# Eight columns of g times w_out's scale: from the end of a VectorE chain to ScalarE

## The chip, the cores and the metric

The kernel runs on one core of a Trainium2 chip. The metric is the device time of one execution in microseconds, as the median of several runs; the kernel before has three. The profile is one more execution of the same program, taken by the hardware profiler. The engines are named as the profile names them: PE is TensorE (PEld its weight loads), DVE is VectorE, ACT is ScalarE, POOL is GpSimd, and SP is SyncE, which issues the transfers here. Every engine takes its own instructions strictly in the order in which the program lists them.

## What is computed

An attention whose keys and values are averaged over blocks of eight rows feeds one dense block with a SoLU and a layer norm in its middle:

```python
k_p = k.reshape(B, H, Sp, 8, D).mean(axis=3)          # B, H, S, D = 8, 8, 576, 64
v_p = v.reshape(B, H, Sp, 8, D).mean(axis=3)
attn = softmax(q @ k_p.T / sqrt(D))
x = (attn @ v_p).transpose(0, 2, 1, 3).reshape(4608, 512)
h = x @ w_in                                          # 512 x 1024
solu = h * softmax(h)
ln = (solu - mean(solu)) / sqrt(var(solu) + 1e-6) * g_ln
out = ln @ w_out                                      # 1024 x 512
```

All inputs and the output are float32. `g_ln` has 1024 values, one for each row of `w_out`, and the kernel multiplies it into `w_out` while that is prepared.

## The kernel before

The 4608 rows are worked in 36 tiles of 128 rows. Products on PE are done in float16, with each operand split into a high and a low float16 part, so that three products (high by high, low by high, high by low) stand for one in float32. A tile passes these stages: the transposed q (`qT`) times the transposed keys (`scores`, PSUM tile `sc`), the softmax, the transposed weights (`eT`) times the values (`av`, PSUM tile `xp`), the split of x (`x_hi` on ACT, `x_lo` on DVE, tile `xT`), the first dense product (`mm1`, L892, PSUM tile `hp`), the SoLU (`h_max` and `h_nb` on DVE, `h_exp` on ACT, `z_mul` on DVE), centring and splitting (`z_hi`, `z_cen` on ACT, `z_lo` on POOL), the transposes by DMA (`zT`), the second dense product (`mm2`, L1024, PSUM tile `op`) and the eviction (`o_evac`, L1032, tile `osb`). The raw keys and values are halved three times on POOL (`pool_kv`, L348, tiles `kr`, `vr`, `kp`, `vp`).

Before the tiles can use `w_out`, it is scaled. `weight("wo", ...)` lists the steps. `w_exp`, `w_shift`, `w_abs` and `w_tail` decode and bound the raw weights. `wo_scale` (from L632) is a chain of small DVE instructions on columns of 128 x 1: it rounds the bounds of w_out and g to powers of two, multiplies them into `pwo` (L637), takes the reciprocal `sw_wo` (L642), changes `pwo` for the use in the evictions (L643), and ends with `sg_wo` (L647). `sg_wo` is g's 1024 values, laid out as 128 partitions by 8 columns (`g_sb`), times the one scale `sw_wo`: column d scales the d-th eighth of `w_out`'s rows. The readers of `sg_wo` are `w_hi` (L667, eight ACT instructions that write the high part of `wo`) and `w_lo` (L696, eight DVE instructions that write the low part from two SBUF tiles, the raw weights and the high part). The first tile's `mm2` needs the high parts first and the low parts in its last third.

The instructions are not placed by a scheduler at build time. `op` numbers every step in the order in which the code lists them, and the table `ORDER` at the head of the file says in which order these numbers are emitted; each engine gets its steps in that order. The numbers do not change with the data.

Three more names come up in what follows. `a_max` (L367, tile `amx_q`) takes the largest magnitude of a batch's q on DVE, and `spread` (L376, PSUM tile `gq`) copies it to all partitions on PE, in the same PSUM buffer that `xp` uses. `hp` has two PSUM buffers, `op` has one.

Of the kernel before, what the change touches and what calls it, by code (L numbers as in the profile page):

```python
# [12 lines left out]
AF = mybir.ActivationFunctionType  # L13
ALU = mybir.AluOpType
# [166 lines left out]
def kernel(  # L181
# [10 lines left out]
    nc = tc.nc  # L192
# [49 lines left out]
    g_sb = const.tile([P, CO], F32, name="g_sb")  # L242
# [1207 lines left out]
```

## Time and profile before

| | us |
|---|---|
| median of 3 runs (lowest, highest) | 484.06 (483.23, 486.1) |
| the profiled execution, whole | 485.99 |
| its span, first to last instruction | 484.3 |
| PE busy in the span | 445.5 (92%) |
| ACT, DVE, POOL busy | 353.9, 346.4, 346.5 |

The span is what the trace covers; 1.69 us of the profiled execution lie outside it. The profiled execution took 1.93 us more than the median of the three runs. PE is the busiest engine by far, so the first question to any other engine's time is whether PE waited for it. The trace tells for each instruction when it began and how long it took, for idle time what ended it, and for each stretch the clock that was granted to PE, as a share of full speed.

### The profile page before, as it was taken

The page shows a single profiled execution, that of the slowest core. Times are in us where ns is not written, and L with a number is a line of the kernel's source. Part 1 is how long each engine was busy: PE and PEld are TensorE (multiplying, and loading weights), DVE is VectorE, ACT ScalarE, POOL GpSimd, SP SyncE. Part 2 cuts the span into 40 slices and gives each one's busy share as a digit, 9 for nine tenths or more (in the row PEclk, how much of TensorE's full clock was granted, in tenths as well). Part 3 has the DMA queues.
Part 4 walks back from the last instruction along what each step waited for, and adds up shares of the span by engine and source line. Part 5 has one row for each costly group of instructions (what it writes and reads, how often), then busy time and mean ns, then how long its engine had stood idle before and what let it go on. Part 6 is the DMA issues. An engine that isn't in the chain of part 4 may idle for free.

```text
span 484.3 us, 9040 instructions
## 1 busy us (share of the span) xinstructions
PE 445.5 (92%) x3100; PEld 231.6 (48%) x3100; DVE 346.4 (72%) x835; ACT 353.9 (73%) x593; POOL 346.5 (72%) x489
## 2 busy tenths in 40 slices
PE   0269869999999999999999999999999999999996
PEld 0124424455455545555555555555545555545462
DVE  3999997679768867777567886688557787782620
ACT  1899769758976597776896689667876679667741
POOL 7254926877999988998889568986999547535340
PEclk9999979999999999999999999999999999999999
DMA  8999934799889989798977988789997656635351
GB/s 277 376 342 222 255 70 103 132 233 231 186 202 233 198 177 223 180 201 223 193 164 182 199 182 199 196 180 211 206 199 154 162 121 120 132 77 137 87 137 59
DMA packets 201390, 89.14 MB, mean 184 GB/s; under 512 B 177664, under 2 KB 186112, under 8 KB 200832
## 3 DMA queue, kind: packets, MB, share of 16 engines
q1 hardware_dynamic: 201344, 88.57, 78.5%
q8 instruction: 24, 0.39, 0.4%
q14 instruction: 22, 0.18, 0.1%
HBM read 36.70 MB, written 9.44 MB: 95 GB/s over the span
## 4 chain that ended last, share of the span: by engine, by line
PE 83%; DVE 6%; ACT 4%; DMA 3%; POOL 2%; issue 1%; SPq 0%; ACTq 0%; DVEq 0%
PE op L1024 36%; PE hp L892 36%; PE xp L860 6%; PE sc L770 3%; DMA qr<-in_q_dram 2%; DVE sg_wo L647 1%; DMA eT<-e 1%; DVE amx_q L367 1%; ACT ab_wi L554 1%; POOL e L839 0%; DVE e L810 0%; ACT u_wi L531 0%; DVE sc L795 0%; ACT sc L791 0%; DVE xT L872 0%
## 5 line engine op out<-in xcount | busy, mean ns | idle before, releaser
L892 PE MATMUL hp<-wi,xT 128*128 128x512 f16 x864 | 198.3, 382 | 2.0 <-ACT xT L868 1.9
L1024 PE MATMUL op<-wo,zT 128*128 128x512 f16 (+1 forms) x888 | 197.0, 373 | 0.8 <-ACT osb L1032 0.6
L892 PEld LDWEIGHTS <-xT 128*128 128x128 f16 x864 | 83.2, 99 | 99.0 <-issue 3.7
L1024 PEld LDWEIGHTS <-zT 128*128 128x128 f16 x888 | 84.7, 98 | 90.7 <-issue 1.0
L959 POOL TENSOR_TENSOR z<-z,z 128x512 f16<-128x512 f32 x71 | 81.9, 1165 | 52.2 <-ACT z L946 51.9
L902 DVE TENSOR_REDUCE m<-hp 128x1 f32<-128x1024 f32 x36 | 44.0, 1222 | 29.6 <-PE hp L892 29.5
L839 POOL TENSOR_TENSOR e<-e,e 128x512 f16<-128x512 f32 x36 | 42.2, 1172 | 23.1 <-ACT e L832 22.9
L348 POOL TENSOR_TENSOR vr<-vr 128x512 f32<-128x512 f32 (+3 forms) x48 | 47.4, 994 | 10.4 <-DMA vr<-in_v_dram 9.7
L951 ACT ACTIVATE z<-z,sz 128x1024 f16<-128x1024 f32 x36 | 41.2, 1145 | 17.7 <-DVE z L937 17.5
L913 ACT ACTIVATE z<-hp,nb,Hb 128x1024 f32<-128x1024 f32 x32 | 38.4, 1198 | 15.5 <-DVE nb L905 14.7
L937 DVE SCALAR_TENSOR_TENSOR z<-hp,rs,z 128x1024 f32<-128x1024 f32 x36 | 46.1, 1280 | 3.7 <-ACT z L913 2.3
L348 POOL TENSOR_TENSOR kr<-kr 128x512 f32<-128x512 f32 (+3 forms) x48 | 40.8, 860 | 3.5 <-DMA kr<-in_k_dram 3.0
L781 DVE TENSOR_REDUCE mx<-sc 128x8 f32<-128x576 f32 x36 | 27.1, 754 | 22.2 <-PE sc L770 21.9
L946 ACT ACTIVATE z<-z,sz 128x1024 f32<-128x1024 f32 x36 | 41.1, 1144 | 0.7
L1032 ACT ACTIVATE osb<-op,f 128x512 f32<-128x512 f32 (+1 forms) x37 | 24.7, 668 | 20.0 <-PE op L1024 12.4
L860 PEld LDWEIGHTS <-vb 128*128 128x128 f16 x640 | 35.3, 98 | 8.5 <-DMA eT<-e 0.7
L860 PE MATMUL xp<-eT,vb 128*128 128x128 f16 (+1 forms) x640 | 38.2, 214 | 0.2 <-DMA eT<-e 0.2
L972 ACT ACTIVATE junk<-z 128x1024 f16<-128x1024 f32 x36 | 37.7, 1047 | 0.2
L751 POOL TENSOR_TENSOR q<-qr,q 128x512 f16<-128x512 f32 x28 | 32.3, 1156 | 7.2 <-ACT q L741 7.2
L795 DVE TENSOR_REDUCE sc<-sc 128x8 f32<-128x576 f32 x36 | 27.4, 762 | 13.5 <-ACT sc L791 13.3
L770 PE MATMUL sc<-kT,qT 128*128 128x72 f16 (+1 forms) x640 | 25.6, 201 | 11.9 <-DMA qT<-q 7.9
L868 ACT ACTIVATE xT<-xp 128x512 f16<-128x512 f32 x36 | 21.3, 592 | 16.5 <-PE xp L860 16.2
(232 smaller groups left out, 588.8 us busy)
## 6 DMA issues: line engine op xcount, KB each, us to landing
kr<-in_k_dram SPq DMA_DIRECT2D x16, 512.0 KB, 4.5
qr<-in_q_dram SPq DMA_DIRECT2D x16, 512.0 KB, 4.8
vr<-in_v_dram SPq DMA_DIRECT2D x16, 512.0 KB, 4.9
out_dram<-osb SPq DMA_DIRECT2D x31, 256.0 KB, 3.3
wor<-in_moe_w_out_dram SPq DMA_DIRECT2D x4, 1024.0 KB, 7.5
wo<-in_moe_w_in_dram SPq DMA_DIRECT2D x2, 1024.0 KB, 9.6
wir<-in_moe_w_in_dram SPq DMA_DIRECT2D x2, 1024.0 KB, 13.2
out_dram<-osb SPq DMA_DIRECT2D x10, 128.0 KB, 2.3
```

The costliest lines, as they stand in the source:

```text
L348: nc.gpsimd.tensor_tensor(out=dst, in0=src[:, :, :n], in1=src[:, :, n : 2 * n], op=ALU.add)
L770: nc.tensor.matmul(sc[lo:hi, h // HB, (h % HB) * SP : (h % HB + 1) * SP], lhsT=t["qT"][:, h, lo:hi], rhs=bat[b]["kT"][:, x, hc], start=(x ...
L839: nc.gpsimd.tensor_tensor(out=m[:, 1], in0=e_pair(i)[:, :, :P], in1=m[:, 0], op=ALU.subtract)
L860: nc.tensor.matmul(xp[:, c, lo:hi], lhsT=vb[b % 2][:, x, c].rearrange("p j d -> p (j d)"), rhs=eT[:, e, lo:hi], start=(n == 0), stop=(n == 3),
L892: nc.tensor.matmul(hp[:, f], lhsT=xT[:, xt, c], rhs=wi[:, wt, c, f * 512 : (f + 1) * 512], start=(part == 0 and n == 0), stop=(part == 2 a ...
L902: nc.vector.tensor_reduce(out=small(i, "m"), in_=tl[i]["hp"], axis=AX.XY, op=ALU.max)
L913: nc.scalar.activation(z, t["hp"], AF.Exp, bias=t["nb"], scale=hsc(i, 0), accum_out=small(i, "se"))
L937: nc.vector.scalar_tensor_tensor(out=t["z"], in0=t["hp"], scalar=t["rs"], in1=t["z"], op0=ALU.mult, op1=ALU.mult, accum_out=small(i, "sz"),)
L946: nc.scalar.activation(t["zf"], t["zf"], AF.Identity, bias=t["sz"], scale=-float(DFF))
L951: nc.scalar.activation(t["z16"][:, 0], t["zf"], AF.Identity, bias=t["sz"], scale=-float(DFF))
L959: eng.tensor_tensor(out=t["z16"][:, 1, fs], in0=t["zf"][:, fs], in1=t["z16"][:, 0, fs], op=ALU.subtract)
L1024: nc.tensor.matmul(op_, lhsT=zT[:, zt, c], rhs=wo[:, wt, c, cols(hf)], start=(part == 0 and n == 0), stop=(part == 2 and n == len(todo) - 1),)
```

## The change

`sg_wo` leaves `wo_scale` and becomes a step of its own, `wo_cols`, on ACT. It reads `g_sb` and the scale `sw_wo`, which `wo_scale` now keeps. All other steps stay as they were. Because there is one step more, every step behind it has a number higher by one in `ORDER`; apart from that and the new step's place the table is the same. The line of the table with the new step (117) and the edits of the code:

```diff
-    299, 300, 302, 225, 301, 259, 483, 484, 345, 344, 260, 123, 347, 303, 227, 485, 486, 146,
+    300, 301, 303, 226, 302, 260, 484, 485, 346, 345, 117, 261, 124, 348, 304, 228, 486, 487,
...
         nc.vector.tensor_scalar(
             out=pwo, in0=pwo, scalar1=-(2.0**-8), scalar2=None, op0=ALU.mult
         )
+        wst["wo"]["sw"] = sw
+
+    def wo_cols():
         sg = const.tile([P, CO], F32, name="sg_wo")
-        nc.vector.tensor_scalar(out=sg, in0=g_sb, scalar1=sw, scalar2=None, op0=ALU.mult)
+        nc.scalar.activation(sg, g_sb, AF.Copy, scale=wst["wo"]["sw"])
         wst["wo"]["s"] = sg
...
-            op("dve", 1.2, t_sum + 0.8, wo_scale, r=[("g2", nm), ("gg2",)], w=[("ws", nm)])
+            n = op("dve", 1.2, t_sum + 0.8, wo_scale, r=[("g2", nm), ("gg2",)], w=[("ws", nm)])
+            op("act", 0.2, t_sum + 2.0, wo_cols, r=[("g",)], w=[("ws", nm)], after=[n])
```

On DVE, at the end of w_out's scale, before (`amx_q` is the magnitude of q, `xT` the split of x, `m` the maximum of a row of `hp`; a number behind a name is its buffer):

```order
L642 RECIPROCAL sw_wo<-pwo 128x1
L643 TENSOR_SCALAR pwo<-pwo 128x1
L647 TENSOR_SCALAR sg_wo<-g_sb,sw_wo 128x8
L367 TENSOR_REDUCE amx_q<-qr_480 128x1
L872 SCALAR_TENSOR_TENSOR xT_670<-xp_653,xT_670 128x512
L902 TENSOR_REDUCE m_684<-hp_556 128x1
```

The same place after:

```order
L642 RECIPROCAL sw_wo<-pwo 128x1
L643 TENSOR_SCALAR pwo<-pwo 128x1
L367 TENSOR_REDUCE amx_q<-qr_480 128x1
L875 SCALAR_TENSOR_TENSOR xT_668<-xp_651,xT_668 128x512
L905 TENSOR_REDUCE m_682<-hp_556 128x1
```

The instruction between `pwo` and `amx_q` is gone, and nothing else moved.

On ACT, at the high parts of w_out, before (`e_1_97` is the split of the softmax, `z_758` the exponentials of the next tile):

```order
L868 ACTIVATE xT_670<-xp_653 128x512
L834 ACTIVATE e_1_97<-e_608 128x2x32
L667 ACTIVATE wo<-wor_370,sg_wo 128x512 x2
L667 ACTIVATE wo<-wor_314,sg_wo 128x512 x2
L667 ACTIVATE wo<-wor_322,sg_wo 128x512 x2
L667 ACTIVATE wo<-wor_282,sg_wo 128x512 x2
L913 ACTIVATE z_758,se_759<-hp_556,nb_694,Hb_362 128x1024
```

The same place after:

```order
L871 ACTIVATE xT_668<-xp_651 128x512
L837 ACTIVATE e_1_97<-e_608 128x2x32
L650 ACTIVATE sg_wo<-g_sb,sw_wo 128x8
L670 ACTIVATE wo<-wor_370,sg_wo 128x512 x2
L670 ACTIVATE wo<-wor_314,sg_wo 128x512 x2
L670 ACTIVATE wo<-wor_322,sg_wo 128x512 x2
L670 ACTIVATE wo<-wor_282,sg_wo 128x512 x2
L916 ACTIVATE z_758,se_759<-hp_556,nb_694,Hb_362 128x1024
```

`sg_wo` stands directly ahead of the first of its readers; PE, POOL and SP have the rows that they had.

## Rows read from the trace of the kernel before

**Rows 1.** Windows: stretch, its length, busy us by engine, PE's clock, DMA share, GB/s

```profile
71.00:110.00 39.00, 38.02 (x296) 19.70 (x295) 27.90 (x68) 29.31 (x52) 27.72 (x40) 1.00 0.73 154
110.00:450.00 340.00, 339.69 (x2422) 177.14 (x2421) 249.43 (x621) 257.44 (x440) 269.73 (x370) 1.00 0.82 180
```

**Rows 2.** Waits of PE: who waited for whom, us in total, times, longest

```profile
PE gq('b', 1)_686 L376 <- DVE xT L872: 5.5, 1, 5.5
```

**Rows 3.** Chain that ended last, 57 to 66 us: start, us, what

```profile
57.35 6.05 DVE sg_wo L647
...
64.52 0.61 DVE xT L872
...
65.17 0.37 PE gq('b', 1)_686 L376 x2
```

**Rows 4.** Timeline of PE, 57 to 83: start, us, instruction, count [idle before, releaser]

```profile
57.80 1.90 PE L892 MATMUL hp<-wi,xT 128*128 128x512 f16 x8 [0.85 <-ACT xT L868]
...
65.34 5.84 PE L892 MATMUL hp<-wi,xT 128*128 128x512 f16 x16
...
75.42 3.62 PE L892 MATMUL hp<-wi,xT 128*128 128x512 f16 x16
...
82.32 1.03 PE L1024 MATMUL op<-wo,zT 128*128 128x512 f16 x4
```

**Rows 5.** Windows around PE's stand, columns as in rows 1

```profile
59.70:63.00 3.30, 0.00 (x0) 0.00 (x0) 3.30 (x1) 0.00 (x0) 3.30 (x6) 1.00 0.98 172
...
65.20:69.80 4.60, 4.60 (x13) 1.76 (x13) 4.57 (x15) 4.60 (x9) 0.00 (x0) 0.50 0.01 4
```

**Rows 6.** Timeline of DVE at the same place, columns as in rows 4

```profile
57.27 6.13 DVE L647 TENSOR_SCALAR sg_wo<-g_sb,sw_wo 128x8 f32<-128x8 f32 x1
```

**Rows 7.** Line L801, an instruction of the same size: ns shortest/median/longest

```profile
L801 DVE TENSOR_SCALAR sc<-sc x36: 154/174/175, 27.5 to 430.4; 128x8 f32<-128x8 f32 x36
```

**Rows 8.** Timeline of POOL, 56 to 66, first and last ones, columns as in rows 4

```profile
56.59 1.14 POOL L839 TENSOR_TENSOR e<-e,e 128x512 f16<-128x512 f32 x1
...
62.12 1.25 POOL L348 TENSOR_TENSOR vr<-vr 128x512 f32<-128x512 f32 x1
...
63.45 0.73 POOL L348 TENSOR_TENSOR vr<-vr 128x256 f32<-128x256 f32 x1
```

**Rows 9.** Timeline of ACT, 57 to 82, columns as in rows 4

```profile
57.64 0.24 ACT L834 ACTIVATE e<-e 128x64 f16<-128x64 f32 x1
63.43 5.25 ACT L667 ACTIVATE wo<-wor,sg_wo 128x512 f16<-128x512 f32 x8 [5.55 <-DVE sg_wo L647]
68.59 1.18 ACT L913 ACTIVATE z<-hp,nb,Hb 128x1024 f32<-128x1024 f32 x1
...
72.11 0.60 ACT L868 ACTIVATE xT<-xp 128x512 f16<-128x512 f32 x1 [1.20 <-PE xp L860]
...
80.86 0.69 ACT L1032 ACTIVATE osb<-op,f 128x512 f32<-128x512 f32 x1 [0.41 <-PE op L1024]
```

**Rows 10.** Line L607, an ACT instruction on three columns, columns as in rows 7

```profile
L607 ACT ACTIVATE Hb<-pw,pv x8: 279/282/297, 34.0 to 410.7; 128x3 f32<-128x3 f32 x8
```

**Rows 11.** Timeline of DVE from 64 to 68, columns as in rows 4

```profile
65.04 1.21 DVE L902 TENSOR_REDUCE m<-hp 128x1 f32<-128x1024 f32 x1
...
67.25 0.73 DVE L696 SCALAR_TENSOR_TENSOR wo<-wor,sg_wo,wo 128x512 f16<-128x512 f32 x1
```

**Rows 12.** Timelines of POOL, DVE and POOL around 457, columns as in rows 4

```profile
456.05 1.16 POOL L959 TENSOR_TENSOR z<-z,z 128x512 f16<-128x512 f32 x1 [8.79 <-ACT z L946]
...
457.05 0.72 DVE L959 TENSOR_TENSOR z<-z,z 128x512 f16<-128x512 f32 x1 [2.80 <-ACT z L946]
...
457.17 1.61 POOL L959 TENSOR_TENSOR z<-z,z 128x512 f16<-128x512 f32 x1
```

**Rows 13.** Timeline of POOL behind its pause, columns as in rows 4

```profile
75.89 2.32 POOL L959 TENSOR_TENSOR z<-z,z 128x512 f16<-128x512 f32 x2 [11.72 <-ACT z L946]
```

276 rows, old and new, of the table ORDER are left out of this document.

## The prediction

> **What bounds the kernel now.** I read the stretches first. From 110 to 450 us PE is busy for 339.69 of 340 us, and from 71 to 110 for 38.02 of 39 [rows 1]. Behind 71 us the kernel therefore ends when PE has got through its list, and the other engines' busy time costs nothing there. What can be won is time by which PE comes into that dense part earlier. The second view is the list of PE's waits: one wait of 5.5 us ended with DVE's `xT` [rows 2]. The third is the chain of waits at that place, which tells what stood ahead of `xT`: `sg_wo` for 6.05 us, then the maximum of q, then `xT`, which ended at 65.13, then PE's `gq` at 65.17 [rows 3]. PE had finished the work in front of it at 57.80 + 1.90 = 59.70 [rows 4], so it stood still for 65.17 - 59.70 = 5.47 us. The fourth view is the granted clock: it was still full in the first 3.3 us of the stand, and when PE went on, from 65.2 to 69.8, it was 0.50, the lower of the two levels, 1.2 GHz [rows 5].
>
> So the one instruction that the change takes from DVE is on the path, and it is a strange one: 6.13 us for 128 x 8 values [rows 6], where another of the same size, 36 times, takes 0.17 [rows 7]. Beside it POOL ran nine further instructions after the one that began at 56.59; each began before the one ahead of it had ended. The last of them ended at 62.12 + 1.25 = 63.37, and the next began at 63.45 [rows 8]. `sg_wo` ended at 63.40, 0.03 us into the first gap. My reading is that this form of DVE instruction can't go on while POOL works without a gap, and that the 6 us are POOL's.
>
> The Trainium skill, "SBUF — State Buffer", section "Who interferes with whom", says that a tensor_scalar between SBUF tiles can use a second port pair that DVE shares with GpSimd under an exclusive lock, and that whoever comes second is blocked for the whole instruction of the other. The trace agrees with the engine that is named, but not with the length: by one instruction the wait would have ended at 56.59 + 1.14 = 57.73 and the change would be worth under 0.5 us, and it lasted for nine more [rows 6, 8]. The sum below goes by the row.
>
> **The change part by part.** *The instruction leaves DVE.* Everything behind it on DVE moves up by 6.05 us [rows 3]: `xT` ends at 65.13 - 6.05 = 59.08. PE is busy until 59.70 [rows 4], so `gq` finds its input there and the whole stand of 5.47 us goes. The last 0.6 us of DVE's gain are hidden behind PE.
>
> *The clock.* At the lower clock 16 products of `hp` took 5.84 us; 16 of the same at full clock, at 75.42, took 3.62 [rows 4]. If PE doesn't stand, nothing that went ahead of the fall is left, and 2.22 us go. Together 7.69 us, which is what the change can bring at most by these rows.
>
> *The instruction on ACT.* Nothing like it is in the trace on eight columns. Below: 0.24 us for 64 columns without a scale from a tile [rows 9]. Above: 0.30 for three columns with one [rows 10]. I take 0.28, the median of the row that is like it in kind. ACT ends the work ahead at 57.64 + 0.24 = 57.88 and then stood idle for 5.55 us until `sg_wo` came [rows 9]; the scale is there before 57.35, when `sg_wo` got the engine in the chain [rows 3]. So it runs from 57.88 to 58.16 in time that was idle. The eight high parts, 68.59 - 63.43 = 5.16 us from the first to what follows, then lie from 58.2 to 63.4 instead of 63.4 to 68.6. PE asks for them after `gq` (0.17), 16 of `hp` (about 3.5) and 16 of `xp` (about 0.9), at 59.70 + 4.57 = 64.3. The new instruction costs nothing at PE; what hides it is a slack of 0.9 us, and without that it would cost its own 0.28.
>
> *What is late next.* ACT moves by 5.2 us, PE could move by 7.69. On the way from 68.59 to the first eviction at 80.86 ACT waited 1.20 and 0.41 us for PE [rows 9]; with PE earlier these go, and the eviction begins at 80.86 - 5.2 - 1.6 = 74.1 and ends at 74.8. The next `op`, which needs that one PSUM buffer, began at 82.32 [rows 4] and could now begin at 82.32 - 7.69 = 74.6. It waits about 0.2 us. From there to 110 us PE was idle for some 1 us of 39 [rows 1]; how much of that comes back or grows with ACT and POOL less far ahead I can't read, 0 to 1 us, and I take 0.2.
>
> *The low parts of w_out against POOL.* This is the one place where the change moves work into a worse neighbourhood. From the start of `h_max` to the first L696 DVE took 67.25 - 65.04 = 2.2 us [rows 11]. `h_max` can now begin at 59.7, so the first L696 comes at 61.9 instead of 67.25, when POOL was idle from 64.17 to 75.89 [rows 8, 13]. At 61.9 POOL is in its run up to 63.37. L696 reads two SBUF tiles. The nearest row is a DVE instruction with two SBUF inputs at the program's end [rows 12]: it began at 457.05 within a POOL instruction that ended at 457.21, took 0.72 us in all, and the POOL instruction that began at 457.17, right behind, took 1.61 us instead of 1.16 (half of 2.32 for a pair [rows 13]). So it waited about 0.2 us, came in between two POOL instructions, and POOL paid 0.45. Bounds for the hold here: 0 if POOL doesn't matter, and 63.37 - 61.9 = 1.5 if it is held as `sg_wo` was, up to the gap. I take 0.3, since the row at 457 is of the same kind. A hold here reaches `z_mul` and through it ACT; `z_mul` waits for `h_exp`, about 1.2 us long from 63.4, and three L696 (0.73 each [rows 11]) with the small instructions between them end, by my estimate, near 64.6, so that nearly all of a hold shows on ACT. It counts as 0.3, and as up to 1.5 in the range.
>
> *Sum.* 5.47 + 2.22 - 0.2 - 0.2 - 0.3 = 7.0 us. Against the profiled execution that is 485.99 - 7.0 = 479.0. That execution lay 1.93 us above the median of the three runs, and the work that is saved is the same in each, so for the median I forecast 484.06 - 7.0 = **477.1 us**.
>
> **The rivals.** *First: the low parts are held as `sg_wo` was.* Then the first L696 costs 1.5 us, and of the last four, which by the same durations run at about 67.4 to 70.1 (an estimate) and with that hold 1.5 later, one or two meet the pair of POOL that stood at 75.89 and comes at about 70: up to 2.3 more [rows 13]. PE asks for the last low part at about 71.3, 1.2 us after DVE would have it without holds, so 1.5 + 2.3 - 1.2 = 2.6 us are lost. That is less than the 3.3 us of stand before which the clock had not yet fallen [rows 5]. The time would be 477.1 + 2.6 = 479.7. For it speaks how long `sg_wo` was held, against it the row at 457. The Trainium skill says in the same section that a DVE instruction with two SBUF inputs contends with a GpSimd instruction that reads SBUF; the row at 457 shows that, at 0.2 us.
>
> *Second: it was the place, not the form.* If something else made DVE stand at 57.3, such as a late input of the work behind, the next instruction inherits it: PE still stands until 65.17 and the time stays at 484.1, with only the 0.28 on ACT moved. Against it: `sg_wo` ended within 0.03 us of POOL's first gap [rows 6, 8], and the chain passes from it to the next instruction without a wait [rows 3].
>
> *Third, slower: the low parts meet a long run of POOL.* Before, they lay in POOL's pause of 11.7 us [rows 13]. If the last four slip behind POOL's restart and are held as long as the longest hold seen, 6.05 us [rows 3], PE stands at the last third of the first `op` for about that, the clock falls again for 2.2, and the first hold of 1.5 comes on top: 9.75 against 7.69, 2.1 us slower, 486.1. It decides from a hold of about 4 us on. Against it: two POOL instructions in a row are 2.3 us, and no instruction with two inputs was held by more than one.
>
> **How the numbers follow.** The forecast, a gain of 5.5 to 8 us, gets 0.72; the first rival 0.13; the second 0.06; the third 0.05; a gain over 8 us, from some wait further on that also goes, 0.04. The range goes from 475.3 (all of 7.69, and the 0.83 us by which the fastest of the three runs lay below the median, rounded down for ACT's waits that vanish) to 481.0 (the first rival with another 1.3 us from the part up to 110 us); the second and third rival and some of the edges lie outside. A change of 0.5%, 2.4 us, is about what a measurement of this kernel can tell from none: faster by more 0.89, within it 0.06, slower by more 0.05.
>
> **What the profile would show.** If the steps are right: DVE goes from `pwo` to the maximum of q at 57.3 without a pause; `sg_wo` stands on ACT at 57.9 and takes 0.24 to 0.30 us; `gq` follows at 59.7, the 16 products behind it take 3.6 us, and the granted clock is full from 57 to 75; the next-largest wait of PE behind 57 us is under 1 us. The first L696 at about 62 shows what POOL costs: 0.73 to 1.0 us by the forecast, above 1.5 by the first rival. Wrong would be a long instruction on DVE at 57.3 under another name, or PE waiting for DVE at the last third of the first `op`, near 71 us.

## The result, and the profile after

| | before | after |
|---|---|---|
| median, us (lowest, highest; runs) | 485.99 (483.23, 486.78; 6) | 480.27 (479.88, 480.91; 6) |
| the profiled execution, whole | 485.99 | 480.81 |
| its span | 484.3 | 479.1 |

The six runs of before include the three of the first table, whose median was 484.06. The ratio of after to before is 0.9897, with a 95% interval from 0.987 to 0.9924: the change makes the kernel about 1% faster. The forecast was 477.1 us. Between the two profiled executions the gain is 5.18 us, where the sum said 7.0.

The stand of PE is gone. PE's timeline (start, us, instruction, count, idle time before it and its releaser) now reads:

```profile
57.69 1.90 PE L895 MATMUL hp<-wi,xT 128*128 128x512 f16 x8 [0.86 <-ACT xT L871]
59.43 0.28 PE L376 MATMUL gq('b', 1)_684<-identb,amx_q 128*128 128x128 bf16 x2
59.54 3.62 PE L895 MATMUL hp<-wi,xT 128*128 128x512 f16 x16
...
68.98 0.22 PE L376 MATMUL gk<-identb,amx_k 128*128 128x128 bf16 x1 [1.25 <-DVE xT L875]
...
76.26 5.34 PE L1027 MATMUL op<-wo,zT 128*128 128x512 f16 x24 [0.16 <-ACT osb L1035]
```

`gq` follows at 59.43 without a wait, and the 16 products behind it take 3.62 us where they took 5.84 [rows 4]: the clock has not fallen. Its windows (columns as in rows 1) show 1.00 on both sides of the place:

```profile
57.00:60.00 3.00, 2.31 (x13) 1.13 (x14) 2.97 (x5) 2.97 (x8) 3.00 (x4) 1.00 1.02 271
60.00:65.00 5.00, 4.95 (x36) 2.56 (x35) 4.96 (x12) 5.00 (x9) 4.65 (x7) 1.00 0.94 192
```

What is new is the 1.25 us ahead of `gk`, the copy of the magnitude of k. The list of PE's waits from 57 to 112 us has it first:

```profile
PE gk L376 <- DVE xT L875: 1.2, 1, 1.2
...
PE xp L863 <- DMA eT<-e: 0.7, 1, 0.7
```

DVE's timeline tells where that comes from. The maximum of q now follows `pwo` at once, and the long instruction has come back a little later as the first low part of `w_out` (L699):

```profile
57.17 1.21 DVE L367 TENSOR_REDUCE amx_q<-qr 128x1 bf16<-128x1024 f32 x1
...
61.11 3.04 DVE L699 SCALAR_TENSOR_TENSOR wo<-wor,sg_wo,wo 128x512 f16<-128x512 f32 x1
...
64.14 1.14 DVE L699 SCALAR_TENSOR_TENSOR wo<-wor,sg_wo,wo 128x512 f16<-128x512 f32 x1
...
65.33 0.73 DVE L699 SCALAR_TENSOR_TENSOR wo<-wor,sg_wo,wo 128x512 f16<-128x512 f32 x1
...
66.39 1.27 DVE L940 SCALAR_TENSOR_TENSOR z<-hp,rs,z 128x1024 f32<-128x1024 f32 x1
```

All eight took 0.73 to 0.75 us before; now the first takes 3.04 and the second 1.14, 2.7 us more together. Beside them POOL's timeline (the pair of halvings at 62.33 shown in two windows, so that its two instructions stand apart):

```profile
61.91 0.45 POOL L348 TENSOR_TENSOR vp<-vr 32x128 f32<-32x128 f32 x1
62.33 1.26 POOL L348 TENSOR_TENSOR vr<-vr 128x512 f32<-128x512 f32 x1
...
63.67 1.06 POOL L348 TENSOR_TENSOR vr<-vr 128x256 f32<-128x256 f32 x1
...
71.00 2.70 POOL L962 TENSOR_TENSOR z<-z,z 128x512 f16<-128x512 f32 x2 [6.27 <-ACT z L949]
```

The first low part ended at 64.14, which is 0.55 us behind the end of POOL's instruction at 63.59; the second ended at 65.28, 0.55 us behind the end of the next one at 64.73. The third came when POOL had stopped and took 0.73. So the low parts were held too, by the end of the same run of POOL.

ACT shows the moved instruction where it was expected, and the other end of the hold:

```profile
57.68 0.29 ACT L650 ACTIVATE sg_wo<-g_sb,sw_wo 128x8 f32<-128x8 f32 x1
58.01 5.30 ACT L670 ACTIVATE wo<-wor,sg_wo 128x512 f16<-128x512 f32 x8
...
67.70 1.15 ACT L954 ACTIVATE z<-z,sz 128x1024 f16<-128x1024 f32 x1 [1.69 <-DVE z L940]
```

### The profile page after: what moved, and what is told of

Same layout as the page of the kernel before. It is cut to its first block, busy times and chain, and to the rows that moved or that the text cites. A ratio compares the mean times of both kernels' runs of the same rounds, so it can differ in the third digit from the quotient of the medians.

```text
span 479.1 us, 9041 instructions
## 1 busy us (share of the span) xinstructions
PE 444.0 (93%) x3100; PEld 230.8 (48%) x3100; DVE 343.2 (72%) x834; ACT 353.9 (74%) x594; POOL 347.1 (72%) x489
## 4 chain that ended last, share of the span: by engine, by line
PE 78%; DVE 8%; ACT 6%; DMA 2%; POOL 2%; issue 2%; SPq 0%; ACTq 0%; DVEq 0%; POOLq 0%
PE op L1027 35%; PE hp L895 34%; PE xp L863 6%; PE sc L773 3%; DMA qr<-in_q_dram 1%; DMA eT<-e 1%; DVE amx_q L367 1%; DVE wo L699 1%; DVE m L905 1%; POOL vb L490 1%; ACT wi L697 1%; DVE z L940 1%; ACT junk L975 1%; DVE wo L564 1%; DVE wor L564 0%
## 5 line engine op out<-in xcount | busy, mean ns | idle before, releaser
L895 PE MATMUL hp<-wi,xT 128*128 128x512 f16 x864 | 196.0, 380 | 2.0 <-ACT xT L871 1.9
```

The lines of the kernel that those rows point to most:

```text
L895: nc.tensor.matmul(hp[:, f], lhsT=xT[:, xt, c], rhs=wi[:, wt, c, f * 512 : (f + 1) * 512], start=(part == 0 and n == 0), stop=(part == 2 a ...
```

## The experiments

**Is it the form or the place?** `sg_wo` stays on DVE, at its place, as eight columns of 128x1.

```diff
-        nc.vector.tensor_scalar(out=sg, in0=g_sb, scalar1=sw, scalar2=None, op0=ALU.mult)
+        for d in range(CO):
+            nc.vector.tensor_scalar(
+                out=sg[:, d : d + 1], in0=g_sb[:, d : d + 1], scalar1=sw, scalar2=None, op0=ALU.mult
+            )
```

> The kernel before, with the eight columns of sg_wo still on DVE at the same place, but as eight instructions of one column (128 x 1) instead of one of 128 x 8. Theory A (the form of the instruction is held while POOL works without a gap; a one-column form is not): the eight take about 1 us in all (0.15 each, overlapping), the maximum of q follows near 58.2, PE does not stand at 59.7, and the time is 4 to 6 us below the kernel before, as with the change. Theory B (it is the place: whatever stands there at 57.3 waits about 6 us): the first of the eight, or the maximum of q, takes over 5 us, and the time is that of the kernel before within 1 us.

Measured: 480.05 us (478.76 to 480.55), ratio 0.9886 (0.9844 to 0.9929). DVE and, beside it, POOL:

```profile
57.58 1.05 DVE L648 TENSOR_SCALAR sg_wo<-g_sb,sw_wo 128x1 f32<-128x1 f32 x8
```

```profile
56.90 1.15 POOL L842 TENSOR_TENSOR e<-e,e 128x512 f16<-128x512 f32 x1
58.01 1.15 POOL L962 TENSOR_TENSOR z<-z,z 128x512 f16<-128x512 f32 x1
```

Eight instructions of 0.20 us ran through in the middle of POOL's run, and the gain was there without ACT. PE stood for 0.41 us ahead of `gq`, since the eight and the maximum of q end later than in after. So it is the form: at this place a 128x8 instruction is held and a 128x1 is not. The second rival (place) falls. The number of values alone isn't it: the 128x8 instruction that the prediction set beside `sg_wo` [rows 7] works in PSUM (`sc`), and in the trace of before 21 of its 36 began and ended within one POOL instruction, none over 0.175 us. `sg_wo` lies in SBUF.

**Another form of the same size.** The product with two SBUF inputs, the scale broadcast to eight columns.

```diff
-        nc.vector.tensor_scalar(out=sg, in0=g_sb, scalar1=sw, scalar2=None, op0=ALU.mult)
+        nc.vector.tensor_tensor(out=sg, in0=g_sb, in1=sw.to_broadcast([P, CO]), op=ALU.mult)
```

> The kernel before, with sg_wo at the same place on DVE as a tensor_tensor of two SBUF inputs (g and the scale spread over eight columns). Theory A1 (an instruction with two SBUF inputs is held like the one before, up to POOL's first gap): it takes about 6 us and ends within 0.1 us of a gap of POOL near 63.4. Theory A2 (a DVE instruction with two SBUF inputs comes in between two POOL instructions, as one did at 457 us in the kernel before): it ends within 1.3 us, when the POOL instruction that runs ends. Theory B (place): 6 us whatever POOL does.

Measured: 483.64 us in one run. The instruction was held, but not to the end of the run (DVE, POOL and PE):

```profile
56.99 3.76 DVE L647 TENSOR_TENSOR sg_wo<-g_sb,sw_wo 128x8 f32<-128x8 f32 x1
```

```profile
60.01 0.71 POOL L348 TENSOR_TENSOR kr<-kr 128x256 f32<-128x256 f32 x1
```

```profile
62.52 0.27 PE L376 MATMUL gq('b', 1)_686<-identb,amx_q 128*128 128x128 bf16 x2 [3.11 <-DVE xT L872]
62.63 5.30 PE L892 MATMUL hp<-wi,xT 128*128 128x512 f16 x16
```

It ended at 60.74, 0.03 us behind the end of one POOL instruction (`kr`, 60.01 to 60.72); the next one of POOL had begun at 60.68. Neither expectation hit the length. That an instruction with two SBUF inputs always gets in at the first end of a POOL instruction, as the row at 457 had suggested [rows 12], is refuted; that a hold of this form always lasts to POOL's next gap is refuted as well.

**Does POOL's run set the end?** In the kernel before, two value halvings that depend on each other, which have a small gap between them, stand earlier in POOL's row.

```diff
-    117, 226, 136, 142, 229, 120, 304, 262, 221, 263, 487, 126, 124, 140, 264, 348, 118, 143,
-    261, 265, 231, 119, 165, 147, 228, 157, 266, 232, 349, 128, 158, 269, 350, 489, 122, 271,
+    117, 226, 157, 158, 136, 142, 229, 120, 304, 262, 221, 263, 487, 126, 124, 140, 264, 348,
+    118, 143, 261, 265, 231, 119, 165, 147, 228, 266, 232, 349, 128, 269, 350, 489, 122, 271,
```

> The kernel before, with only POOL's order changed: the two dependent halvings of the values (vr, 128x512 and 128x256), which ended POOL's run, stand about 2 us earlier in it, so that the pause of 0.08 us between them comes near 61.5 instead of 63.4. Theory A (held up to POOL's first gap): sg_wo ends at that gap, near 61.5, and takes about 4.2 us instead of 6.13; PE stands about 3.6 us instead of 5.47; the time falls by 1.9 us, or by up to 4 if the clock then doesn't fall. Theory B (place) and the rule that the wait ends with the one POOL instruction that runs: sg_wo keeps 6.1 us, and the time stays.

Measured: 484.03 us, ratio 0.9983 (0.9954 to 1.0013). DVE, POOL and PE:

```profile
57.26 4.22 DVE L647 TENSOR_SCALAR sg_wo<-g_sb,sw_wo 128x8 f32<-128x8 f32 x1
```

```profile
60.19 2.06 POOL L348 TENSOR_TENSOR vr<-vr 128x512 f32<-128x512 f32 x2
62.20 0.73 POOL L348 TENSOR_TENSOR kr<-kr 128x256 f32<-128x256 f32 x1
```

```profile
63.24 0.37 PE L376 MATMUL gq('b', 1)_686<-identb,amx_q 128*128 128x128 bf16 x2 [3.56 <-DVE xT L872]
63.41 6.50 PE L892 MATMUL hp<-wi,xT 128*128 128x512 f16 x16
```

The hold moved with POOL's pair, to the length that was expected (4.2 us), and PE's stand with it (3.6). The time did not follow. The clock fell all the same, and the 16 products took 6.50 us, 0.66 more than in the profile of before [rows 4]; and the kernel before itself can have a short hold, as its next profiles show.

**How long is the hold in other executions?** The kernel before, unchanged, in two more profiles.

> The kernel before, profiled once more. If the hold always lasts to POOL's first pause, sg_wo takes 6.1 us again within 0.1 us. If it can end at a boundary between two POOL instructions, which of them being chance, it takes another time, such as the 3.8 us that it took with the fill of PE, and ends with one of POOL's instructions all the same.

> The kernel before in one more profile, for the length of the hold. Theory (which boundary between POOL's instructions lets the product in differs from execution to execution): it takes either about 3.8 us, ending behind kr, or about 6.1 us, ending at the pause behind vr. Rival (the 6.13 us of the first profile was the odd one out and the hold is always short): 3.8 us a third time, and a time near 482.5.

The first of the two, DVE, POOL and PE (482.44 us whole, span 480.7):

```profile
57.17 3.81 DVE L647 TENSOR_SCALAR sg_wo<-g_sb,sw_wo 128x8 f32<-128x8 f32 x1
```

```profile
60.24 0.71 POOL L348 TENSOR_TENSOR kr<-kr 128x256 f32<-128x256 f32 x1
60.92 0.86 POOL L348 TENSOR_TENSOR kp<-kr 128x128 f32<-128x128 f32 x2
```

```profile
62.75 0.27 PE L376 MATMUL gq('b', 1)_686<-identb,amx_q 128*128 128x128 bf16 x2 [3.16 <-DVE xT L872]
62.86 3.62 PE L892 MATMUL hp<-wi,xT 128*128 128x512 f16 x16
```

The second (486.75 us, span 485.0):

```profile
57.24 6.08 DVE L647 TENSOR_SCALAR sg_wo<-g_sb,sw_wo 128x8 f32<-128x8 f32 x1
```

```profile
65.09 0.37 PE L376 MATMUL gq('b', 1)_686<-identb,amx_q 128*128 128x128 bf16 x2 [5.42 <-DVE xT L872]
65.26 6.05 PE L892 MATMUL hp<-wi,xT 128*128 128x512 f16 x16
```

The same program in front of the same row of POOL instructions was held for 3.81 us once and for 6.1 us twice. With the short hold PE's stand was 3.16 us, the clock stayed full, and the execution took 4.3 us less than the second one. The rival that the long hold was an exception is refuted. The kernel before lies between 479.9 and 487.6 us in 73 runs (median 484.4), where 22 runs of after lie between 479.3 and 481.7 (median 480.3). Of the runs of before whose mean granted clock is on record, those at 0.998 or above took 479.9 to 483.4 us, and those at 0.996 or below 482.5 to 487.6. That the length of the hold makes this spread is inferred from that and from the three traces; the other runs have none.

**What does the fall of the clock cost?** The kernel before with 24 products ahead of `gq`, so that PE doesn't stand.

```diff
+    def pe_fill():
+        t = ps_o.tile([P, DM], F32, tag="o", name="fill")
+        for n in range(24):
+            nc.tensor.matmul(t, lhsT=minus, rhs=wi[:, 0, 0, :DM], start=True, stop=True)
...
         for n in order:
+            if n == 483:
+                pe_fill()
             ops[n][3](*ops[n][4])
```

> The kernel before with sg_wo as it is, and 24 products of 512 columns on PE, whose result nobody reads, in the 5.47 us in which PE stood (24 x 0.216 = 5.2 us, into the op buffer that is still free). Theory: the granted clock stays full, the 16 products of hp behind the stand take 3.62 us instead of 5.84, and the time falls by about 2.2 us although DVE's 6 us are still there. Rival: PE would have to wait for ACT and DVE anyway, the 2.2 us come back as a wait before 80 us, and the time stays within 0.7 us.

Measured: 484.03 us, ratio 0.9981 (0.9954 to 1.0007), where 2.2 us less was expected. In the trace the clock stayed at 1.00 and the 16 products took 3.62 us. But in this execution too the hold was short (3.78 us), and the kernel before kept its clock behind such a hold without a fill, so this trace alone doesn't show what the fill does. The runs do: in all ten the mean granted clock was 0.998 to 1.0, where 16 of the 19 runs of the kernel before beside them had 0.991 to 0.996. That the time didn't fall with it fits the fill's fixed 5.3 us, longer than the stand that it covers behind a short hold. The time is the one that the rival wrote, but the wait that it named, before 80 us, isn't in the trace. So the clock's price is shown by the products (3.62 against 5.30 to 6.50 us), not by this run's time. A stand of 3.11 us (the form with two inputs) had a fall of the clock behind it and one of 3.16 had none, so the stand's length alone doesn't tell.

**What holds the low parts?** The kernel after once more, and then without the two value halvings at the end of POOL's run.

```diff
         for n in order:
-            ops[n][3](*ops[n][4])
+            if n not in (158, 159):
+                ops[n][3](*ops[n][4])
```

> The changed kernel as it is, as the measure for the two that run beside it. Both theories: 480 us within 1 us, the first low part of w_out held to POOL's pause near 63.6 us, some 2.5 to 3 us long, and PE's wait for xT of about 1.2 us at gk.

> The changed kernel without the first two halvings of one batch's values on POOL (that part of the values is left out of the sum), which are the last 2.3 us of POOL's run. Theory: the first low part is released near 62.4 instead of 63.6, the second takes its normal 0.73 us instead of 1.14, together about 1.6 us less hold; PE's wait at gk is under 0.2 us, and the time is 1 to 1.5 us below the changed kernel. Rival (it is not POOL): the first low part still takes about 3 us.

Measured: after 480.37 us (479.69 to 481.73), ratio 0.9919 (0.9888 to 0.9949), its first two low parts 2.91 and 1.14 us, `gk` waiting 1.34. Without the pair, and so with an incomplete result: 478.39 us (478.33 to 479.22), ratio 0.9879 (0.9829 to 0.993), 2.0 us less than after, where 1 to 1.5 were expected. DVE and PE of the run without it:

```profile
60.90 1.83 DVE L699 SCALAR_TENSOR_TENSOR wo<-wor,sg_wo,wo 128x512 f16<-128x512 f32 x1
...
62.72 0.73 DVE L699 SCALAR_TENSOR_TENSOR wo<-wor,sg_wo,wo 128x512 f16<-128x512 f32 x1
```

```profile
67.30 0.22 PE L376 MATMUL gk<-identb,amx_k 128*128 128x128 bf16 x1
```

The second low part is free, the first ends 0.55 us behind POOL's last instruction (62.18), and `gk` doesn't wait. So POOL's pair is what held the low parts there. Its price by the two profiles is 1.3 to 1.5 us: the second `op` begins at 74.43 instead of 75.97, and the spans are 476.7 and 478.0. Where the rest of the 2.0 us between the medians comes from is open; the pair's own work is gone too, and the first low part is still 1.1 us longer than free.

**Can the low parts be moved out of POOL's way?** First by DVE's order: the first low part stands behind the maximum of k, `z_mul` comes next, and the other low parts come behind it.

```diff
-    147, 118, 227, 137, 143, 230, 121, 305, 263, 222, 264, 488, 127, 125, 141, 265, 349, 119,
-    144, 262, 266, 232, 120, 166, 148, 229, 158, 267, 233, 350, 129, 159, 270, 351, 490, 123,
-    272, 149, 352, 126, 271, 128, 331, 122, 353, 275, 274, 306, 489, 273, 150, 234, 307, 223,
+    147, 118, 227, 137, 143, 230, 121, 305, 263, 222, 264, 488, 127, 265, 266, 141, 349, 144,
+    262, 232, 166, 148, 125, 267, 119, 229, 158, 233, 350, 351, 120, 129, 123, 126, 128, 122,
+    159, 270, 490, 272, 149, 352, 271, 331, 353, 275, 274, 306, 489, 273, 150, 234, 307, 223,
```

> The changed kernel with another order on DVE alone: the first low part stands behind the maximum of k, in the time in which DVE waits for h_exp anyway, and z_mul comes before the second low part instead of behind the third; the x split stands behind the second. Theory (the low parts that POOL holds are what the change lost): z_mul begins near 64.6 instead of 66.39, PE's wait of 1.25 us at gk goes, and the time is 1 to 2 us below the changed kernel. Rival (what was lost lies elsewhere, or POOL holds the later low parts against z_lo): the wait moves to the last third of the first op, near 71 us, and the time is that of the changed kernel within 0.5 us or above.

Measured: 481.75 us (481.25 to 483.6), ratio 0.9949 (0.9922 to 0.9977), 1.4 us slower than after. DVE, POOL and PE:

```profile
66.92 5.86 DVE L699 SCALAR_TENSOR_TENSOR wo<-wor,sg_wo,wo 128x512 f16<-128x512 f32 x6
```

```profile
69.12 3.11 POOL L962 TENSOR_TENSOR z<-z,z 128x512 f16<-128x512 f32 x2 [4.62 <-ACT z L949]
```

```profile
72.84 1.46 PE L1027 MATMUL op<-wo,zT 128*128 128x512 f16 x6 [1.48 <-DVE wo L699]
...
77.48 4.69 PE L1027 MATMUL op<-wo,zT 128*128 128x512 f16 x21 [1.46 <-ACT osb L1035]
```

The wait at `gk` went, and two others of 1.5 us came: because everything was earlier, POOL's pair for `z` was earlier too, at 69.12, and met the last low parts. Six of them took 5.86 us where six free ones would take 4.1 (an estimate from 2.72 for four, in after). The first one, at 62.16, was still held (1.76 us). The rival was right: the hold was moved, not removed.

Then by POOL's order: a tiny POOL instruction that reads DVE's `rs`, which is moved behind the third low part (step 266), so that the pair of halvings waits until three low parts are done.

```diff
-    144, 262, 266, 232, 120, 166, 148, 229, 158, 267, 233, 350, 129, 159, 270, 351, 490, 123,
+    144, 262, 232, 120, 266, 166, 148, 229, 158, 267, 233, 350, 129, 159, 270, 351, 490, 123,
...
+    stay = const.tile([P, 1], F32, name="stay")
...
         for n in order:
+            if n == 158:
+                nc.gpsimd.tensor_tensor(out=stay, in0=tl[1]["rs"], in1=phalf, op=ALU.mult)
             ops[n][3](*ops[n][4])
```

> The kernel after, with one more instruction of 128x1 on POOL ahead of the pair of value halvings (vr, 62.33 2.41 us in the profile of after): it reads rs, which VectorE now makes behind the third low part of w_out, so POOL's run ends at about 62.2 and the pair starts only when the three low parts are done. Nothing is left out. Theory (the end of POOL's run sets when the low parts get in, and the pair has room before POOL's next work at 71.0): the first low part ends at about 62.7 as without the pair, the third by about 64.3, the pair lies in about 64.3 to 66.9, gk does not wait for VectorE, and the time is that of the run without the pair, about 478.4 us, 2.0 under after. Rival (the pair then meets z_mul or the next four low parts and holds those, or its late end holds the value chain): gk or the next op waits over 1 us and the time is 480 us or more.

> The kernel after once more, beside the one before it. Both theories: 480.3 us within 0.5; the first low part takes 2.9 to 3.1 us and gk waits 1.2 to 1.4 us, as in its two profiles, since POOL's run ends with the vr pair each time.

Measured: 481.18 us (478.86 to 482.47), ratio 0.9925 (0.9892 to 0.9959), against 480.02 for after beside it, ratio 0.9899 (0.9858 to 0.9939); in that one the low parts took 3.03 and 1.14 us and `gk` waited 1.46. DVE, POOL, ACT and PE with the tiny instruction:

```profile
62.19 1.36 DVE L700 SCALAR_TENSOR_TENSOR wo<-wor,sg_wo,wo 128x512 f16<-128x512 f32 x1
...
68.44 3.64 DVE L700 SCALAR_TENSOR_TENSOR wo<-wor,sg_wo,wo 128x512 f16<-128x512 f32 x4
```

```profile
65.28 2.08 POOL L349 TENSOR_TENSOR vr<-vr 128x512 f32<-128x512 f32 x2
70.30 2.79 POOL L963 TENSOR_TENSOR z<-z,z 128x512 f16<-128x512 f32 x2 [2.94 <-ACT z L950]
```

```profile
73.62 1.20 ACT L917 ACTIVATE z<-hp,nb,Hb 128x1024 f32<-128x1024 f32 x1 [1.18 <-DVE nb L909]
```

```profile
76.76 5.34 PE L1028 MATMUL op<-wo,zT 128*128 128x512 f16 x24 [1.08 <-ACT osb L1036]
```

`gk` no longer waits, as the theory had it; and the last four low parts met the pair for `z`, 0.92 us longer than free, which reached the second `op` through ACT, as the rival had it. So also that pair was made to wait, by one more tiny instruction.

```diff
+            if n == 274:
+                nc.gpsimd.tensor_tensor(out=stay, in0=wo[:, 1, 2, :1], in1=phalf, op=ALU.mult)
```

> The run before last with the pair of value halvings behind the third low part, and one more instruction of 128x1 on POOL ahead of its z pair (L963, 70.30 there) that reads the last of the four low parts, so that this pair too starts only when VectorE is through with them. Nothing is left out. Theory (each low part of w_out is held only by POOL instructions that run while it wants in; with both POOL runs out of its way nothing is left on the path): the four low parts take 2.7 to 2.8 us instead of 3.64, ScalarE's wait for nb (1.18) falls to 0.3 or less, the op behind (1.08 for osb) waits 0.3 or less, and the time is 1 us under the 481.2 of that run or better: 479 to 480.3 us, 0.988 to 0.991 of the kernel before. Rival (the z pair starts later and is itself on the path, through zT and f to osb): the op after next waits for zT or osb by as much as was won, and the time stays at 481 us, 0.9925.

Measured: 480.09 us (479.23 to 480.94), ratio 0.9916 (0.9883 to 0.9948). DVE, POOL and PE:

```profile
61.77 0.88 DVE L700 SCALAR_TENSOR_TENSOR wo<-wor,sg_wo,wo 128x512 f16<-128x512 f32 x1
...
67.69 2.73 DVE L700 SCALAR_TENSOR_TENSOR wo<-wor,sg_wo,wo 128x512 f16<-128x512 f32 x4
```

```profile
62.06 0.90 POOL L349 TENSOR_TENSOR vp<-vr 32x128 f32<-32x128 f32 x1
```

```profile
82.14 2.12 PE L1028 MATMUL op<-wo,zT 128*128 128x512 f16 x9 [0.99 <-DMA zT<-z]
```

and the queue of SP, which issues the transposes:

```profile
76.58 1.34 SPq L453 DMA_TRANSPOSE kT<-k  x1
78.02 5.22 SPq L971 DMA_TRANSPOSE zT<-z  x2
```

The last four low parts are free, the first two nearly so, and from `gq` to the end of the second `op` PE waits for nothing. Then, at 82.14, it waits 0.99 us for `zT`. SP issued that transpose at 78.02, right behind the one of the keys, 4.1 us before PE went on; in after SP issued it at 78.80, PE came to it at 82.44 and didn't wait. So a part of what was won at the low parts was lost again at this transpose. Whether it was late by its place in SP's queue or because it took longer (in this stretch `zT` took 3.1 us from issue to landing in the median, 2.8 in after) is open. Both sides were half right. The time, 480.09 us, is 1.1 us below that of one tiny instruction, as the theory had it, but the ratios to the runs of before beside them, 0.9916 and 0.9925, can't be told apart, and 0.9916 lies just outside what the theory wrote. Nor can 480.09 be told from after (480.0 to 480.4): no version that computes the whole result is shown to beat the kernel after. In the profiles of both versions with tiny instructions the work ahead of the place was later (the eight products of `hp` began at 58.77 and 58.35, in three profiles of after at 57.69, 57.53 and 58.45). Whether that comes from the edit is open; from that point to the end the last version took 419.7 us, and after 420.5 to 421.6.

## Why the prediction was right and where it wasn't

**The stand and the clock: right.** Both terms came as computed: 5.47 us of stand gone, and 2.22 us of the 16 products. With eight columns of 128x1, which leave the rest as it was, the same stand goes but for 0.41 us, so it was this one instruction. That POOL held it is shown by its end, which moved with POOL's pair. One count in the reading is off: behind the POOL instruction that began at 56.59 there were eight further ones up to 63.37, not nine; nothing in the sum hangs on it.

**The instruction on ACT: right.** 0.29 us at 57.68, where 0.28 at 57.88 was written, in time that was idle; it costs PE nothing.

**ACT late at the first eviction: right.** PE waits 0.16 us there (0.2). Of the stretch behind, 0.2 was taken: the wait for `eT` has grown from 0.2 to 0.65 us, and between 110 and 450 us PE is idle for 0.6 us instead of the 0.31 of [rows 1]. It is 0.7 to 0.8 rather than 0.2, inside the bounds of 0 to 1; why `eT` comes later is open.

**The low parts against POOL: this is the step that failed, in its size.** The mechanism was named, and bounded by 0 and 1.5 us; 0.3 was taken, "since the row at 457 is of the same kind". The hold was 2.3 us on the first low part and 0.4 on the second. Two things made it longer than the upper bound: the first low part came at 61.11 and not at 61.9, and behind the first gap of POOL, to which the bound counted, the second low part met another instruction. At PE it came out as 1.25 us ahead of `gk`. From the eight products of `hp` to the second `op` PE gained (82.32 - 57.80) - (76.26 - 57.69) = 5.95 us of the 7.69, so 1.7 us were lost up to there, the 0.16 at the eviction included, where 0.5 was written. The row at 457 misled: it showed an instruction that happened to ask 0.16 us before POOL's instruction ended. It was let in at the first end of a POOL instruction, which the form does not guarantee, as 3.0 and 2.9 us for the low part, and 3.76 for `sg_wo` with two inputs, show. The sentence "no instruction with two inputs was held by more than one" was true of the trace of before and not of after: the first low part, from 61.11 on, was held over the two of `kp`, `vp` and the first of `vr`.

**The first rival is the case that came**: 479.7 us was written for it, by 1.5 us at the first low part and 2.3 at the last four. The first part came, larger. The second didn't, because POOL's pair for `z` was itself later (71.00), behind ACT's 1.69 us of wait for `z_mul`. The last low part had begun before it, and this time POOL paid: its pair took 2.70 us, 2.32 in before [rows 13]. The hold of the last low parts came with the other order on DVE and with one tiny instruction. The rival reckoned with no fall of the clock because the 2.6 us were less than the 3.3 of [rows 5]; a stand of 3.11 us had a fall behind it in one run here.

**The base: the second step that failed.** The prediction said that "the work that is saved is the same in each" execution, and so took 7.0 us from the median. The hold that is saved is 3.8 us in one execution and 6.1 in another. By the profile with the short hold the change is worth 482.44 - 480.81 = 1.6 us, by the profile of [rows 3] 5.2, and between the medians of all runs 484.4 - 480.3 = 4.1. That after lies so close together, and before doesn't, is part of the gain.

**What luck there was.** Of the 3.2 us between 477.1 and 480.27, the profiles account for 1.8 (479.0 was written for after, and it took 480.81), and the base for the other 1.4. The measured time lies in the range because the range left room above the first rival's 479.7, not because the sum was right in these two places.

The Trainium skill, "SBUF — State Buffer", section "Who interferes with whom", says that a DVE instruction with two SBUF inputs contends with a GpSimd instruction that reads SBUF. The traces agree: the first low part was held for 2.3 us, where the forecast had taken 0.3 by the row at 457.

## What to carry to other kernels

When a VectorE instruction takes many times what its size asks for, look whether it runs beside an unbroken row of GpSimd instructions, and whether a form that isn't held (here 128x1 columns, or the same product on ScalarE) can take its place. Then ask at once which instruction comes next into the same row: the gain stops there. Pushing the work or the GpSimd row aside passed the hold on to the next meeting in two of three tries, and in the third PE waited for a transpose instead. A gain that is read from one profile needs a second profile of the same kernel, since the length of such a hold differs from one execution to the next.

## What the runs showed of the hardware

In every profile a held instruction ended at a fixed time behind the end of some POOL instruction: `sg_wo` 0.03 us behind (63.40 after 63.37, 61.47 after 61.44, 60.98 after 60.95), a low part of 128x512 0.55 us behind (64.14 after 63.59, 62.73 after 62.18, 62.65 after 62.10). So it gets in when a POOL instruction ends, but not at each one: `sg_wo` was passed over at up to eight ends (57.74 to 62.15 in before), and let in at the next. The gap between two halvings that depend on each other (0.08 us in before and after) let in whatever was still held there, every time. The step from `kr` to `kp`, where POOL shows no gap, let it in three times (3.76 us with two inputs, 3.78 and 3.81) and not in the two profiles with 6.13 and 6.08 us. When DVE got in ahead of `vp` in the last version, `vp` took 0.90 us instead of 0.45, so the two engines hold each other. Not held at all beside POOL were the 128x1 columns and the 128x8 instruction in PSUM. What decides at which step DVE gets in was not found.
